# Delta rule and MLP on one core: squares of two chunks, one V scaling and three weight exponents at other places of the start-up

## The chip, the core and the metric

The kernel runs on one core of a Trainium2 chip. The core has five engines that work side by side, each through its own list of instructions in order: TensorE (PE, matmuls, and PEld for its weight loads), VectorE (DVE), ScalarE (ACT), GpSimd (POOL) and SyncE (SP), whose queue issues most of the DMA transfers. They wait for each other on semaphores. The metric is the device time of one execution in microseconds (us).

## The reference

All arrays are float32. The first half is a delta rule over 768 time steps for 4 batches of 8 heads with head size 48; its output is laid out as 3072 tokens of 384 numbers and goes through an MLP with the exact GELU.

```python
k_n = k / (np.linalg.norm(k, axis=-1, keepdims=True) + 1e-06)
for t in range(S):                       # S = 768
    y[:, :, t] = np.einsum('bhd,bhde->bhe', q[:, :, t], state)
    v_old = np.einsum('bhde,bhd->bhe', state, kt)
    state = state + bt * np.einsum('bhd,bhe->bhde', kt, vt - v_old)
x = y.transpose(0, 2, 1, 3).reshape(3072, 384)
h = x @ w_in                             # 384 x 2048
out = (0.5 * h * (1.0 + erf(h / sqrt(2)))) @ w_out   # 2048 x 384
```

The caller hands `moe_w_in` and `moe_w_out` over as 64-bit floats; the kernel makes 32-bit floats of their bits itself.

## The kernel before

**Tiling.** The 768 steps are cut into 12 chunks of 64. A *unit* is one chunk of two batches (128 partitions: two batches by 64 steps; 8 heads along the free axis), so a chunk has two units. Chunks go in pairs, called groups: group 0 is chunks 0 and 1, group 1 is chunks 2 and 3. `first` holds the four units of group 0, `third` the two of chunk 2, `fourth` the two of chunk 3.

**One group.** K is transposed on PE (`transposed`, copied to SBUF by ACT as Kt), its Gram matrices are made (`grams`, PE; copied by ACT as G and diag), and for every head a triangular system of 64 rows is inverted: 32-row diagonal blocks by row steps on DVE (`eliminate_steps`, lines 442 and 444: 60 short instructions for one group), the off-diagonal block by two small products (`join`, psJ on PE). The result is Zf. Its halves are written by DVE transposes (L457), by ACT copies (L499), and the quarters that must be zero by memsets on POOL (L466), the first of them by ACT (L464). The norms of K come from sums of squares: by DVE for group 0, and for group 1 by `sum_of_squares` (L291): one ACT instruction for each unit and head that squares 128x48 numbers and adds them up along the way. `prep` takes the root of these sums on POOL (L306, `pow`), `finish_both` (DVE) makes factors of them.

**One chunk.** `against_state` makes the right-hand side W (for chunk 0 from V alone, on POOL, L562; later with psK from PE), `solve` multiplies it by Zf (psU on PE, copied to U by ACT, L603), `use` makes the output and the state's update (psY on PE), `read` copies the output to x (ACT, L636, four instructions for a unit), `next_state` adds the update to the state St (DVE, L629), `turn` transposes x on PE for the MLP (copied by ACT as xT, L660). `queries` makes the products of Q and K, called P; for chunks 0 and 1 `masked` (POOL, L405) masks them. `scale_v` (POOL, L332) multiplies V by the norms of K.

**The MLP.** `fc1` makes a 128-column group of the hidden layer (psH, L677: six matmul instructions on PE) and its GELU on ACT (L679, tile G); there are 16 such groups for a chunk and two PSUM buffers for them. `fc2` is the second layer (psO, L690); from chunk 2 on it is done in seven products (L715).

**The weights.** They come in 16 parts, eight of w_in and eight of w_out. Part n is decoded in four steps, five DVE instructions and one ACT instruction: `begin(n)` (DVE, L218) takes the exponent bits, `exponents(n)` (ACT, L223) clamps and scales them, `mantissas(n)` (DVE, L228 and L230) makes the mantissas, `signed(n)` (DVE, L235 and L236) joins both and releases the raw buffer, on which `fetch` (SP, L210) loads a later part. The raw parts of w_in lie in w_out's space (four buffers), those of w_out in three others; the exponents (w_e) have two buffers.

**What sets the order.** Up to the first `next_state` everything is written out by hand: there the order of the calls in the program is the order on every engine. Behind that, steps get a due time in units of a chunk (`plan`); DVE keeps exactly that order, and on the other engines a planner places the instructions by its own estimates. The hand-written part is, in short: loads; squares, transposes and diagonals of group 0; Grams of group 0; transposed Q and queries of the four units; transposes and Grams of chunks 2 and 3; the row steps (which run on DVE all that while); `against_state` and the four masks on POOL; the joins, with the DVE transposes between them; then V of chunk 1 is scaled and the first parts of the weights are decoded around `solve`, `use` and `read` of chunk 0.

In the planned part the 32 sums of squares are due from 1.08 to 1.5, among the weights' parts 3 to 10 and the hidden layer of chunk 0. For chunk 3, K lies twice in SBUF: in Kp, where it is loaded late, and in Qp[2] and Qp[3], where it is loaded early for the transposes.

Of the kernel before, what the change touches and what calls it, by code (L numbers as in the profile page):

```python
# [8 lines left out]
F32 = mybir.dt.float32  # L9
# [3 lines left out]
ACT = mybir.ActivationFunctionType  # L13
# [3 lines left out]
def kernel(  # L17
# [28 lines left out]
    nc = tc.nc  # L46
# [152 lines left out]
    def fetch(n):  # L199
        if n >= len(w_parts):  # L200
            return
        dst, src = w_parts[n]
        if n < n_in:
            raw = stage[:, n % NS * 2 * WG:(n % NS + 1) * 2 * WG]
        else:
            raw = slots[(n - n_in) % len(slots)]
        w_raw[n] = raw.rearrange("q (n w) -> q n w", w=2)
        raw = raw.rearrange("q (m n w) -> q m n w", m=dst.shape[1], w=2)
        for m in range(dst.shape[1]):
            nc.sync.dma_start(out=raw[:, m], in_=src[:, m])  # L210
# [10 lines left out]
    def exponents(n):  # L221
        e = halves[n][3]
        nc.scalar.activation(e, e, ACT.Relu, bias=lim[:, 0:1], scale=float(2 ** 23))  # L223

    def mantissas(n):
        dst, lo, hi, e = halves[n]
        bits = dst.bitcast(U32)
        nc.vector.tensor_scalar(bits, hi, 0xFFFFF, 0x100000, op0=ALU.bitwise_and,  # L228
                                op1=ALU.bitwise_or)
        nc.vector.scalar_tensor_tensor(dst, lo, 2.0 ** -32, bits, ALU.mult, ALU.add)  # L230
# [52 lines left out]
    def sum_of_squares(u, h):  # L283

        if "both" not in ns:
            n23 = wk.tile([128, 2 * NA, H], F32, tag="n0", name="n0", bufs=1)
            ns[2], ns[3] = n23[:, 0:NA], n23[:, NA:]
            ns["both"] = n23
        if h == 0:
            u.ksq = wk.tile([128, H, D], F32, tag="ksq", name="ksq")  # L290
        nc.scalar.activation(u.ksq[:, h], u.Kn[:, h, 0:D], ACT.Square,  # L291
                             accum_out=ns[u.c][:, u.a, h:h + 1])

    def prep(c):
# [36 lines left out]
    def scale_v(u, engine=nc.gpsimd):  # L331
        engine.tensor_tensor(u.V, u.V, ns[u.c][:, u.a].unsqueeze(2).to_broadcast([128, H, D]),  # L332
                                op=ALU.mult)

    def transposed(u, part=(0, 1)):
        for x in part:
            if x == 0:
                dst = u.Kt = wk.tile([128, 2, NP, C], F32, tag="Kt", name="Kt", bufs=6)
            elif u.c == 1:
                dst = u.Qt = su.tile([128, 2, NP, C], F32, tag="Qt1", name="Qt1")  # L340
            else:
                dst = u.Qt = wk.tile([128, 2, NP, C], F32, tag="Qt", name="Qt")
            psT = sq("psT", NP, 128)
            flat = (Qp[2 + u.a] if u.c == 3 and x == 0 else (u.Kp, u.Qp)[x]).rearrange("q h d -> q (h d)")
            for j in range(NP):
                nc.tensor.transpose(psT[:, j, :], flat[:, j * 128:(j + 1) * 128], ident)
            nc.scalar.copy(dst.rearrange("q p j n -> q j p n"),
                           psT.rearrange("q j (p n) -> q j p n", p=2))
# [23 lines left out]
    def grams(us):  # L372
        g = us[0].c // 2
        psG = products(us, 0)
        if us[0].t == 0:
            Gs[g] = (wk if g else su).tile([128, NU, HB], F32, tag="G", name="G", bufs=1)
        span = slice(us[0].t * H, (us[-1].t + 1) * H)
        nc.scalar.copy(heads(Gs[g][:, span]), psG[:, :, :, HB:C])
        if g > 0:
            if us[0].t == 0:  # L380
                Ds[g] = wk.tile([128, NU, HB], F32, tag="diag", name="diag", bufs=1)
            nc.scalar.copy(heads(Ds[g][:, span]), psG[:, :, :, 0:HB])
            for p in range(2):
                lower = slice(p * C + HB, (p + 1) * C)
                nc.scalar.copy(Ds[g][lower, span], Gs[g][lower, span])
# [3 lines left out]
    def queries(us):  # L389
        c = us[0].c  # L390
        psP = products(us, 1)
        if c not in Ps:
            Ps[c] = (su if c == 1 else wk).tile([128, NA * H, C], F32, tag=f"P{c == 1}", name="P",
                                                bufs=1)
        for u in us:
            u.P = Ps[c][:, u.a * H:(u.a + 1) * H]
        dst = heads(Ps[c][:, us[0].a * H:(us[-1].a + 1) * H])
        if c < 2:
            nc.scalar.copy(dst, psP)
        else:  # L400
            both = mask.unsqueeze(1).to_broadcast([128, len(us) * H, C])
            nc.vector.tensor_tensor(dst, psP, heads(both), op=ALU.mult)  # L402
# [411 lines left out]
    def signs(c0, c1):  # L814
        psB = sq("psB", c1 - c0, B * H)
        for c in range(c0, c1):
            nc.tensor.transpose(psB[:, c - c0, :], bt[:, c].rearrange("n p t -> n (p t)"),
                                ident[0:B * H, 0:B * H])
        for p in range(2):
            src = psB[HALF[p]].rearrange("q c (a p h) -> q c a p h", p=2, h=H)[:, :, :, p, :]  # L820
            nc.scalar.mul(beta_m[HALF[p], c0:c1], src, -1.0)
# [27 lines left out]
    for u in first:  # L849
        grams([u])  # L850
    signs(2, NC)
    for u in first:
        transposed(u, (1,))
        queries([u])
    for a in range(NA):
        fetch_in(tiles[2, a].Qp[:, :, 0:D], q, tiles[2, a])
# [1 line left out]
        fetch_in(Qp[2 + a][:, :, 0:D], k, tiles[3, a])  # L858
    for n in range(2, NS):
        fetch(n)  # L860
    for n in range(n_in, n_in + len(slots)):
        fetch(n)
    load_v(1)
    third = [tiles[2, a] for a in range(NA)]
    for u in third:
        transposed(u, (0,))
    grams(third)
    for u in third:
        transposed(u, (1,))
    fourth = [tiles[3, a] for a in range(NA)]  # L870
    for u in fourth:
        transposed(u, (0,))
    grams(fourth)
    for fn, *args in rows:
        fn(*args)
    nc.vector.scalar_tensor_tensor(ng, gms[0][:, 0:NA], -1.0, ns[0], ALU.mult, ALU.mult)
    back0[0](*back0[1:])
    against_state(first[:NA])
    for u in first:
        masked(u)  # L880
    back1[0](*back1[1:])
    for a in range(NA):
# [1 line left out]
    back2[0](*back2[1:])  # L884
    for a in range(NA):
        join(0, (a,), 1)
    for u in first[NA:]:
        scale_v(u)
    begin(0)
    exponents(0)  # L890
    mantissas(0)
    begin(1)
    mantissas(1)
    solve(first[:NA])
    exponents(1)
    signed(0)
    use(first[:NA])
    for u in first[:NA]:
        read(u)
    signed(1)  # L900
    for u in first[:NA]:
        turn(u)
    for u in first[:NA]:
        update(u)
    begin(2)
    exponents(2)
    mantissas(2)
    signed(2)
    for u in first[:NA]:
# [7 lines left out]
    def late():  # L917
# [3 lines left out]
        for a in range(NA):  # L921
# [3 lines left out]
            for c in range(5, NC, 2):  # L925
# [4 lines left out]
    plan += [at(0.98, 0.985, [(1.0, load, 3)]),  # L930
             at(1.02, 1.1, [(1.0, join, 0, range(NA, 2 * NA), level) for level in range(2)]),
]
    sums = [(1.0, sum_of_squares, tiles[c, a], h) for c in (2, 3) for a in range(NA) for h in range(H)]
    plan += [at(1.08, 1.5, sums), at(1.51, 1.511, [(1.0, prep, c) for c in (2, 3)]), at(1.65, 1.655, [(1.0, finish_both)]), at(2.97, 2.971, [(1.0, finish, 4)]), at(2.675, 2.676, [(1.0, queries, third)]),
             at(1.12, 1.6, state_steps(1)),
             at(1.75, 2.45, eliminate_steps(1)),
             at(2.58, 2.74, join_steps(1)), at(2.72, 2.98, state_steps(2)),
# [75 lines left out]
```

## Time and profile before

Six runs had a median of 671.13 us (670.78 to 671.65).

| | |
|---|---|
| profiled execution, its own time | 670.97 us |
| its span | 669.3 us |
| mean granted clock of TensorE | 0.985 |
| PE busy | 642.4 us, 96% |
| DVE busy | 451.5 us, 67% |
| ACT busy | 229.3 us, 34% |
| POOL busy | 82.2 us, 12% |
| chain that ended last | PE 84%, DVE 10%, ACT 2% |

The shares are means over the whole span, and the stages differ. In the order of time:

| us | stage | DVE busy | ACT busy | POOL busy | PE busy |
|---|---|---|---|---|---|
| 47.00 to 51.80 | joins end, first parts decoded | 4.73 | 3.96 | 4.21 | 2.64 |
| 51.80 to 57.00 | solve, outputs of chunk 0 | 5.08 | 4.99 | 0.00 | 3.53 |
| 57.00 to 62.13 | turn, update, first MLP group | 4.12 | 2.38 | 0.00 | 5.13 |
| 62.13 to 88.00 | hidden layer of chunk 0, parts 3 to 8 | 24.73 | 20.41 | 6.18 | 23.86 |
| 88.00 to 117.00 | parts 8 to 15, second layer of chunk 0 | 28.48 | 11.79 | 0.00 | 27.21 |

From 120 us to the end PE is busy 99% of the time. In the lines shown below, a row of the order of time has its start, its length, the engine, the line, the operation with the tiles it writes and reads and their sizes, and how many instructions are merged in the row; a bracket at the end is the idle time of the engine before it and what ended that. Starts of instructions on one engine can lie a little before the end of the one ahead, since they are pipelined.

### The profile page before, as it was taken

Reading aid. Unit: us, or ns where it says so; the run is one execution under the profiler, and the core shown is the slowest. Engines: PE = TensorE matmul, PEld = TensorE weight load, DVE = VectorE, ACT = ScalarE, POOL = GpSimd, SP = SyncE. Lnnn points to the kernel's source line nnn. Section 1 sums busy time; section 2 is a strip of 40 time slices with the busy share of each in tenths; the row PEclk is TensorE's granted clock in tenths of the full one; section 3 lists DMA queues with packets and bytes.
Section 4 is the critical chain, followed back from the end, with each engine's and each line's share of the span. In section 5 each row is a group of like instructions: output and inputs, shape, how many; then the busy total and the mean of one; then the engine's idle time right before and its main releaser. Section 6 shows DMA issues by size and latency. Waiting matters only on the chain.

```text
span 669.3 us, 21705 instructions
## 1 busy us (share of the span) xinstructions
PE 642.4 (96%) x9542; PEld 560.7 (84%) x9542; DVE 451.5 (67%) x921; ACT 229.3 (34%) x605; POOL 82.2 (12%) x82
## 2 busy tenths in 40 slices
PE   6868998999999999999999999999999999999997
PEld 5656775866789989989989989989989989989997
DVE  6999999994699846489846479845479844324021
ACT  3367754714342143142143142143142133122220
POOL 4050300104011021111021111021111010000000
PEclk9976999999999999999999999999999999999999
DMA  9786656203431232511332511212301210100101
GB/s 130 178 252 172 118 171 134 48 0 69 81 50 37 49 51 43 87 27 32 55 50 48 85 26 28 52 21 34 65 3 24 56 19 3 24 2 2 24 1 25
DMA packets 158431, 39.76 MB, mean 59 GB/s; under 512 B 150016, under 2 KB 153216, under 8 KB 158336
## 3 DMA queue, kind: packets, MB, share of 16 engines
q1 hardware_dynamic: 152464, 33.40, 26.3%
q10 hardware_dynamic: 5872, 4.97, 3.2%
q8 instruction: 75, 1.23, 0.8%
q14 instruction: 20, 0.16, 0.1%
HBM read 33.62 MB, written 4.72 MB: 57 GB/s over the span
## 4 chain that ended last, share of the span: by engine, by line
PE 84%; DVE 10%; ACT 2%; issue 2%; DMA 1%; SPq 0%; DVEq 0%; ACTq 0%
PE psH L677 36%; PE psX L715 12%; PE psY L715 12%; PE psZ L715 4%; PE psO L690 4%; PE psK L572 3%; PE psJ L517 3%; PE psG L367 3%; PE psU L597 2%; PE psY L615 2%; DVE tmp L442 2%; DVE Nu L444 2%; DVE w_e L235 1%; PE psY L624 1%; DVE w_out_sb L236 1%
## 5 line engine op out<-in xcount | busy, mean ns | idle before, releaser
L677 PE MATMUL psH<-xT,w_in_sb 128*128 128x256 f32 x1152 | 262.2, 384 | 1.8 <-ACT G L679 1.7
L677 PEld LDWEIGHTS psH<-xT,w_in_sb 128*128 128x128 f32 x1152 | 216.0, 191 | 33.3 <-ACT G L679 3.3
L679 ACT ACTIVATE G<-psH 128x256 f32<-128x256 f32 x192 | 73.5, 383 | 180.2 <-PE psH L677 168.2
L444 DVE TENSOR_TENSOR Nu<-Nu,tmp 128x30 f32<-128x30 f32 (+9 forms) x180 | 62.9, 349 | 6.2
L442 DVE TENSOR_TENSOR tmp<-Nu 128x30 f32<-128x30 f32 (+9 forms) x180 | 60.5, 336 | 5.1
L715 PE MATMUL psX<-w_out_sb,G 128*128 128x192 f32 x320 | 56.2, 329 | 0.0
L715 PE MATMUL psY<-w_out_sb,G 128*128 128x192 f32 x304 | 54.2, 329 | 0.6
L715 PEld LDWEIGHTS psX<-w_out_sb,G 128*128 128x128 f32 x320 | 52.2, 190 | 0.7
L715 PEld LDWEIGHTS psY<-w_out_sb,G 128*128 128x128 f32 x304 | 49.1, 190 | 2.1 <-DVE u L761 1.8
L690 PE MATMUL psO<-w_out_sb,G 128*128 128x384 f32 x128 | 45.4, 496 | 1.6 <-DVE w_out_sb L236 1.6
L660 ACT COPY xT<-psX 128x384 f32<-128x384 f32 x24 | 11.4, 478 | 102.6 <-PE psX L659 101.5
L306 POOL TENSOR_TENSOR n<-n,half 128x16 f32<-128x16 f32 x10 | 29.4, 2938 | 86.4 <-DVE n L281 65.4
L690 PEld LDWEIGHTS psO<-w_out_sb,G 128*128 128x128 f32 x128 | 23.0, 190 | 17.3 <-DVE w_out_sb L236 4.0
L603 ACT COPY U<-psU 64x192 f32<-64x192 f32 x96 | 30.1, 314 | 20.6 <-PE psU L597 19.4
L402 DVE TENSOR_TENSOR P<-psG,mask 128x1024 f32<-128x1024 f32 x10 | 12.2, 1224 | 34.9 <-PE psG L367 34.9
L466 POOL MEMSET Zf<- 32x512 f32 x23 | 12.4, 540 | 154.1 <-DVE Zf L457 153.2
L724 DVE TENSOR_TENSOR S<-G 128x512 f32<-128x512 f32 x20 | 13.7, 687 | 25.8 <-ACT G L679 25.7
L580 DVE TENSOR_TENSOR W<-psK,V 128x384 f32<-128x384 f32 x22 | 12.2, 553 | 28.1 <-ACT y L579 28.1
L332 POOL TENSOR_TENSOR V<-V,n 128x384 f32<-128x384 f32 x18 | 17.3, 964 | 108.0 <-DMA V<-in_v_dram 95.4
L638 DVE TENSOR_TENSOR x<-psY,y 64x192 f32<-64x192 f32 x80 | 28.2, 353 | 0.9
L715 PE MATMUL psY<-T,G 128*128 128x192 f32 x160 | 28.2, 329 | 0.0
L715 PE MATMUL psX<-T,G 128*128 128x192 f32 x160 | 28.1, 329 | 0.0
(138 smaller groups left out, 869.0 us busy)
## 6 DMA issues: line engine op xcount, KB each, us to landing
Kp<-in_k_dram SPq DMA_DIRECT2D x76, 96.0 KB, 3.6
w_out_sb<-in_moe_w_in_dram SPq DMA_DIRECT2D x24, 256.0 KB, 3.8
V<-in_v_dram SPq DMA_DIRECT2D x48, 96.0 KB, 3.0
out_dram<-o_sb ACTq DMA_DIRECT2D x46, 96.0 KB, 2.2
w_raw<-in_moe_w_out_dram SPq DMA_DIRECT2D x10, 384.0 KB, 5.3
Zf<-in_moe_w_out_dram SPq DMA_DIRECT2D x6, 384.0 KB, 6.6
Qp<-in_q_dram SPq DMA_DIRECT2D x64, 32.0 KB, 2.2
Qp<-in_q_dram SPq DMA_DIRECT2D x16, 96.0 KB, 3.9
```

What stands on the lines that cost most here:

```text
L306: nc.gpsimd.tensor_tensor(flat, flat, half, op=ALU.pow)
L367: nc.tensor.matmul(psG[HALF[p], r, i * NP + j, :], lhsT=u.Kt[rows, p, j, :], rhs=(u.Qt if x else u.Kt)[rows, p, j, :], start=True, stop=True)
L442: nc.vector.tensor_tensor(tmp, nu[:, j + 1:, j:j + 1].to_broadcast([128, n, j]), nu[:, j:j + 1, 0:j].to_broadcast([128, n, j]), op=ALU.mult)
L444: nc.vector.tensor_tensor(nu[:, j + 1:, 0:j], nu[:, j + 1:, 0:j], tmp, op=ALU.add)
L517: nc.tensor.matmul(psJ[to, i, :], lhsT=(xm if level else off)[rows, u, :], rhs=zf[rows, u, HB:C] if level else xm[rows, u, :], start=True, ...
L572: nc.tensor.matmul(u.psK[to, x, r, j, :], lhsT=(u.Qt if x else u.Kt)[rows, p, j, :], rhs=St[rows, u.a, p, j, :], start=True, stop=True)
L603: copy(pairs(u.U[HALF[p]], s), u.psU[HALF[p ^ s], p])
L638: nc.vector.tensor_tensor(dst, src, pairs(u.y[HALF[p ^ s]], s), op=ALU.add)
L677: nc.tensor.matmul(psH, lhsT=w_in_sb[:, f // 2, m, f % 2 * 128:(f % 2 + 1) * 128], rhs=xTs[c][:, m, :], start=(m == 0), stop=(m == NM - 1))
L679: nc.scalar.activation(G[:, f, :], psH, ACT.Gelu)
L690: nc.tensor.matmul(u.psO, lhsT=G[:, f, u.a * 128:(u.a + 1) * 128], rhs=w_out_sb[:, f, :], start=(f == 0), stop=(f == NF - 1))
L715: nc.tensor.matmul(ps_, lhsT=lhs[:, f, :], rhs=rhs[:, f, :], start=first and f == 0, stop=f == FH - 1, skip_group_check=not first)
```

## The change

Three things are placed elsewhere:

- The 32 sums of squares of chunks 2 and 3 go from the planned part into the hand-written one: eight of chunk 2 between the transposes and the queries of the last two units of `first` (four for each), eight behind the transposes of chunk 2's K, and the sixteen of chunk 3 behind chunk 3's Grams. Those of chunk 3 read K from Qp[2] and Qp[3]. Their sums lie in a tile that takes turns with another (`root` in place of `n0`).
- V of chunk 1 is scaled on POOL between the masks of chunk 0 and those of chunk 1, so before the memsets of Zf. Its loads go out ahead of the first loads of w_out.
- `exponents(1)` stands ahead of `solve` on ACT; `begin(2)` stands behind `signed(0)` on DVE, and `exponents(2)` between the reads of the two units of chunk 0.

In the planned part the instructions of the other engines fall in another order behind that. On ACT the exponents of part 8 stand behind the GELUs of groups 11, 12 and 13; before, behind 11 and 12. On PE one matmul pair of group 11 comes between the two halves of psU of chunk 1.

```diff
     def sum_of_squares(u, h):
         if "both" not in ns:
-            n23 = wk.tile([128, 2 * NA, H], F32, tag="n0", name="n0", bufs=1)
+            n23 = wk.tile([128, 2 * NA, H], F32, tag="root", name="n23", bufs=1)
...
-        nc.scalar.activation(u.ksq[:, h], u.Kn[:, h, 0:D], ACT.Square,
+        kn = Qp[2 + u.a] if u.c == 3 else u.Kn
+        nc.scalar.activation(u.ksq[:, h], kn[:, h, 0:D], ACT.Square,
                              accum_out=ns[u.c][:, u.a, h:h + 1])
...
+    third = [tiles[2, a] for a in range(NA)]
+    some = iter([(u, h) for u in third for h in range(H)])
     for u in first:
         transposed(u, (1,))
+        for i in range(4 if u.t > 1 else 0):
+            sum_of_squares(*next(some))
         queries([u])
...
     for n in range(2, NS):
         fetch(n)
+    load_v(1)
     for n in range(n_in, n_in + len(slots)):
         fetch(n)
-    load_v(1)
-    third = [tiles[2, a] for a in range(NA)]
     for u in third:
         transposed(u, (0,))
+    for left in some:
+        sum_of_squares(*left)
     grams(third)
...
     grams(fourth)
+    for u in fourth:
+        for h in range(H):
+            sum_of_squares(u, h)
     for fn, *args in rows:
         fn(*args)
...
-    for u in first:
+    for u in first[:NA]:
+        masked(u)
+    for u in first[NA:]:
+        scale_v(u)
+    for u in first[NA:]:
         masked(u)
...
-    for u in first[NA:]:
-        scale_v(u)
     begin(0)
     exponents(0)
     mantissas(0)
     begin(1)
     mantissas(1)
+    exponents(1)
     solve(first[:NA])
-    exponents(1)
     signed(0)
+    begin(2)
     use(first[:NA])
-    for u in first[:NA]:
-        read(u)
+    read(first[0])
+    exponents(2)
+    read(first[1])
     signed(1)
...
-    begin(2)
-    exponents(2)
     mantissas(2)
     signed(2)
...
-    sums = [(1.0, sum_of_squares, tiles[c, a], h) for c in (2, 3) for a in range(NA) for h in range(H)]
-    plan += [at(1.08, 1.5, sums), at(1.51, 1.511, [(1.0, prep, c) for c in (2, 3)]), ...
+    plan += [at(1.51, 1.511, [(1.0, prep, c) for c in (2, 3)]), ...
```

More of the change, by code (lines that the diff above doesn't have):

```diff
@@ L932 @@
 ]
-    sums = [(1.0, sum_of_squares, tiles[c, a], h) for c in (2, 3) for a in range(NA) for h in range(H)]
-    plan += [at(1.08, 1.5, sums), at(1.51, 1.511, [(1.0, prep, c) for c in (2, 3)]), at(1.65, 1.655, [(1.0, finish_both)]), at(2.97, 2.971, [(1.0, finish, 4)]), at(2.675, 2.676, [(1.0, queries, third)]),
+    plan += [at(1.51, 1.511, [(1.0, prep, c) for c in (2, 3)]), at(1.65, 1.655, [(1.0, finish_both)]), at(2.97, 2.971, [(1.0, finish, 4)]), at(2.675, 2.676, [(1.0, queries, third)]),
              at(1.12, 1.6, state_steps(1)),
```

## The prediction

> **What bounds the kernel now.** I read the page's chain of work that ended last, then the same chain piece by piece from 36 to 122 us, then the order of time of each engine there. From 119.88 us to the end the chain is TensorE almost without a break, work that the change doesn't touch, so what it moves must show before that. There the chain ends like this (start, length, what):
>
> ```profile
> 115.12 0.88 DVE w_e L235
> 116.02 0.97 DVE w_out_sb L236
> 117.03 2.85 PE psO L690 x8
> 119.88 2.59 PE psH L677 x12
> ```
>
> VectorE (DVE) decodes the weights to 116.98 us; eight matmuls wait for the last part. From 62.13 DVE has next to no gap, so whatever moves a DVE step there moves the end by the same amount. Its losses, from the order of time on DVE (start, length, engine, line; the bracket is the idle time before and what ended it):
>
> ```profile
> 47.49 0.96 DVE L228 TENSOR_SCALAR w_in_sb<-w_out_sb 128x768 uint32<-128x768 uint32 x1
> 49.83 1.19 DVE L228 TENSOR_SCALAR w_in_sb<-w_out_sb 128x768 uint32<-128x768 uint32 x1
> 51.05 1.47 DVE L230 SCALAR_TENSOR_TENSOR w_in_sb<-w_out_sb,w_in_sb 128x768 f32<-128x768 uint32 x1
> 56.76 0.55 DVE L228 TENSOR_SCALAR w_in_sb<-w_out_sb 128x768 uint32<-128x768 uint32 x1
> 59.22 0.96 DVE L235 SCALAR_TENSOR_TENSOR w_e<-w_out_sb,w_e 128x768 uint32<-128x768 uint32 x1 [0.91 <-ACT w_e L223]
> 87.99 0.96 DVE L235 SCALAR_TENSOR_TENSOR w_e<-Zf,w_e 128x768 uint32<-128x768 uint32 x1 [0.57 <-ACT w_e L223]
> ```
>
> Two waits for exponents on ScalarE (ACT), 0.91 and 0.57, and three steps longer than alone (0.55 and 0.96) beside GpSimd (POOL). The reader should see that at most some 3 us can be won. The work of ACT and POOL around it:
>
> ```profile
> 43.20 1.24 ACT L385 COPY diag<-G 32x512 f32<-32x512 f32 x2
> 47.28 0.63 ACT L464 ACTIVATE Zf<-low 32x512 f32<-32x512 f32 x1 [2.83 <-DVE Zf L457]
> 50.79 2.64 ACT L603 COPY U<-psU 64x192 f32<-64x192 f32 x8 [0.40 <-PE psU L597]
> 53.46 0.94 ACT L223 ACTIVATE w_e<-w_e,lim 128x768 uint32<-128x768 uint32 x1
> 65.78 0.23 ACT L291 ACTIVATE ksq<-Kp 128x48 f32<-128x48 f32 x1
> 67.14 0.37 ACT L679 ACTIVATE G<-psH 128x256 f32<-128x256 f32 x1
> 86.47 0.66 ACT L679 ACTIVATE G<-psH 128x256 f32<-128x256 f32 x2
> 87.02 0.94 ACT L223 ACTIVATE w_e<-w_e,lim 128x768 uint32<-128x768 uint32 x1
> 88.51 0.38 ACT L679 ACTIVATE G<-psH 128x256 f32<-128x256 f32 x1 [0.55 <-PE psH L677]
> 41.17 4.97 POOL L405 TENSOR_TENSOR P<-P,mask 128x512 f32<-128x512 f32 x4
> 47.30 2.18 POOL L466 MEMSET Zf<- 32x512 f32 x3 [1.16 <-DVE Zf L457]
> 49.56 2.14 POOL L332 TENSOR_TENSOR V<-V,n 128x384 f32<-128x384 f32 x2
> ```
>
> **The squares.** Six run from 65.78 to 67.14, 0.227 us each with their accumulator reads; 32 are moved. Two groups of four go between a Qt copy and a P copy of ACT, where it idles 1.25 us: 0.91 fits, no cost. Eight go behind the Kt copies, whose next free start is 33.97: they end at 35.79, and the G copy that started at 35.28 and all that alternates with TensorE behind it comes 0.51 later. The last sixteen stand behind the last diagonal copies, free at 44.33 (+0.51 = 44.84), and take 3.63, to 48.47. But the zeroing of Zf (L464), behind them in ACT's order, started at 47.28, on the chain. **It comes 1.19 late**; ACT had 2.83 idle here, and the squares need more. The joins on DVE may start some 0.2 later through the 0.51; the slack below covers that.
>
> **Exponents sooner.** ACT's order is now the Zf copies, exponents 0 and 1, U, the reads of the first unit, exponents 2, the other reads. Exponents 0 start at 49.45 + 1.19 = 50.64; from one to the next start is 0.84 (53.46 to 54.30), so U starts at 52.32 (psU is ready at 50.77 + 1.19 = 51.96), 1.53 late. U takes 2.67 to the next start: 54.99; four reads 1.30 (half of 54.30 to 56.91): 56.29; exponents 2: 57.13; four reads: 58.43. Before, the reads ended at 56.91: **TensorE's turn, update and first MLP group start 1.52 late**, the group at 59.66 + 1.52 = 61.18.
>
> On DVE the 0.91 wait goes: signed(2) is reached near 58.2 and exponents 2 are ready at 57.23. What is late next is the state sum L629, which waits for the update's end, 59.73 + 1.52 = 61.25. DVE is there, one sum done, at about 60.65 and waits 0.6. The next part begins near 61.77 against 62.13: of the 0.91 only **0.36** is won here.
>
> **V between the masks.** POOL does the same work in another order: two masks to 43.66, V to 45.80, two masks to 48.28, three memsets to about 50.5. The overlap cost DVE 0.40 (beside a memset) + 0.63 + 0.52 (beside V) = 1.55. Now DVE's first decode step meets a mask and the next ones memsets. No row shows that meeting; the bounds are 0, and 1.24 for a step held for a whole mask. I take 0.64, as beside V, the nearest row, and 0.40 for each of two memsets: 1.44, a gain of 0.1, swallowed by the 0.6 of slack at the state sum; a loss of up to 0.6 would be, too. The first memset ends near 49.0, before psU's start, 48.76 + 1.19 = 49.95. V's DMAs are issued from 34.13 instead of 39.08, ahead of six weight loads on SyncE's (SP's) queue; they landed 6.1 to 7.4 us after issue, so the first pair by about 42 and the second by 44.5, needed at 43.66 and 44.73. The weight loads issue some 4 us later and are first read at 84.94: free.
>
> [...]
>
> **From 62 to 88 us.** The 7.3 us of squares leave ACT, so TensorE loses its waits for Gelu outputs (0.86, 0.31, 0.50). Its new course, by lengths of the old: the first MLP group, 2.72 at half clock, to 63.90; joins 1.13; two groups of 1.345, to 67.72; a group with joins 2.48; three groups, to 74.23; psK 2.01; four groups 5.38, to 81.62. That is 1.02 ahead of the old 82.64. But the changed order of ACT puts exponents 8 behind *three* Gelus after U, not two. psU with a third of a group between its halves ends for U at 81.62 + 1.21 + 0.45 = 83.28; the first Gelu comes 2.62 after that, 85.90; the third group starts 0.44 later (it needs that buffer), its Gelu 1.60 later at 87.94, exponents 8 at 88.22, and DVE's step 0.97 later, at **89.19**. It stood at 87.99. DVE, ready at 87.06, waits 2.1 us instead of 0.57. Behind it DVE has no gap to give back up to 116.98, and TensorE, ahead of it, still waits there.
>
> Sum: no other term reaches the end, which moves by 89.19 - 87.99 = **+1.20 us**. Against the profiled execution's own 670.97 us (span 669.3 and 1.7 around it) that is 672.17; that execution lay 0.16 under the median of 671.13, so 672.3.
>
> **The clock is the open term.** The granted clock was 0.50 from 45.2 to 62.10, then 1.00. TensorE had been busy without a gap since 56.94, 5.2 us. I let the rise come 1.52 later with the same work (63.62). In the other rise, at 41.65, half clock had lasted only 3.3 to 3.4 us: that soon after 58.43 the rise comes at 61.8, and half of 1.8 us is saved: +0.3. Twice that stretch gives 65.2: +2.0. [...]
>
> **Rivals.**
> - *The rise is early and the shift nearly hidden:* +0.0 to +0.6, 671.1 to 671.7. For it: the short stretch before 41.65. Against: 5.2 us the second time.
> - *The rise is late, or V lands late:* each makes TensorE's chain longer. +1.8 to +2.4, 672.9 to 673.5. V costs only once the second pair lands past about 45.5, since the memset has 0.9 to spare; against it 7.4 at most in the trace.
> - *Faster:* the squares hide wholly in ACT's idle 2.83. If they ended before 47.28, the chain would not be late, and DVE would win 0.91 + 0.57 and most of V's 1.15: 668.5 to 669.7. It decides below 0.15 us a square in place of 0.227; the row speaks against it. That the exponents aren't the last thing DVE waits for is in the forecast.
>
> **How the numbers follow.** Forecast (+0.6 to +1.8) 0.50; early rise 0.20; late 0.20; faster 0.10. A measurement of this kernel can hardly tell less than 0.2%, 1.34 us, from no change. The forecast's part above +1.34 is 0.20 and joins the late case: slower 0.40; the rest of it and the early case: same 0.50; faster 0.10. The range 670.9 to 673.3 leaves out the fast case and the ends of the late one.
>
> **What would show it.** The Zf zeroing on ACT near 48.5 directly behind squares; U near 52.3; no wait at signed(2), one of about 0.6 at L629; then TensorE without Gelu waits from 64 to 75; a wait of some 2 us on DVE for L223 near 87 to 89; the last w_out step at about 118.2. Wrong if exponents 8 come in time: then the DVE wait near 87 is short and the end is early. Wrong the other way if POOL holds psU (memset past 50) or squares wait for their DMAs.

## The result, and the profile after

The changed kernel took 673.02 us (median of 19 runs, 672.10 to 674.36), the kernel before 671.02 (39 runs): a ratio of 1.0029, 95% interval 1.0023 to 1.0035. It is slower by 2.0 us. The range on record (670.9 to 673.3) holds that. The likeliest outcome, within 0.2%, is not what came; slower by over 0.2% had a chance of 0.4.

The profiled execution after took 673.26 us (span 671.5), 2.29 more than the one before. The fences below show single rows of a view; rows between them are left out. The chain of waits of the changed kernel, in order of time (start, length, what):

```profile
48.56 0.63 ACT Zf L465
...
87.76 1.58 PE psH L678 x6
...
89.74 0.83 ACT w_e L223
90.60 0.97 DVE w_e L235
...
118.62 0.97 DVE w_out_sb L236
119.63 2.85 PE psO L691 x8
122.48 2.59 PE psH L678 x12
```

The last decode step starts at 118.62 where it stood at 116.02. DVE's step for part 8 moved just as much, from 87.99 to 90.60, and everything behind it kept its distance: psO follows 29.03 after that step (29.04 before). Back from that step the chain runs over ACT and TensorE without a break to the zeroing of Zf at 48.56. So the question of the whole study is what sets the step of part 8. In the order of time of the changed kernel, ACT:

```profile
48.56 0.63 ACT L465 ACTIVATE Zf<-low 32x512 f32<-32x512 f32 x1
50.74 1.76 ACT L223 ACTIVATE w_e<-w_e,lim 128x768 uint32<-128x768 uint32 x2
52.52 2.64 ACT L604 COPY U<-psU 64x192 f32<-64x192 f32 x8
...
84.71 2.59 ACT L604 COPY U<-psU 64x192 f32<-64x192 f32 x8 [1.55 <-PE psU L598]
87.32 0.66 ACT L680 ACTIVATE G<-psH 128x256 f32<-128x256 f32 x2
89.36 0.38 ACT L680 ACTIVATE G<-psH 128x256 f32<-128x256 f32 x1 [1.38 <-PE psH L678]
89.64 0.93 ACT L223 ACTIVATE w_e<-w_e,lim 128x768 uint32<-128x768 uint32 x1
```

Zf's zeroing has lost its idle 2.83 in front and starts at 48.56 instead of 47.28: squares stand directly ahead of it. Further down, the exponents of part 8 are behind a third Gelu, which itself waits 1.38 for TensorE. TensorE in the same view:

```profile
61.39 2.93 PE L678 MATMUL psH<-xT,w_in_sb 128*128 128x256 f32 x6
64.25 1.44 PE L485 MATMUL psJ<-XM,G 32*32 32x32 f32 x64
...
82.66 0.68 PE L598 MATMUL psU<-W,Zf 64*64 64x48 f32 x32
83.27 0.70 PE L678 MATMUL psH<-xT,w_in_sb 128*128 128x256 f32 x2
83.90 0.68 PE L598 MATMUL psU<-W,Zf 64*64 64x48 f32 x32
...
87.76 1.56 PE L678 MATMUL psH<-xT,w_in_sb 128*128 128x256 f32 x6 [0.82 <-ACT G L680]
```

The first hidden-layer group starts 1.73 later than before (59.66) and runs wholly at half clock (0.50 until 64.86). psU starts at 82.66, where it was before (82.64), but is split around a pair of group 11. The kernel before, TensorE and ACT:

```profile
59.66 2.79 PE L677 MATMUL psH<-xT,w_in_sb 128*128 128x256 f32 x6
82.64 1.15 PE L597 MATMUL psU<-W,Zf 64*64 64x48 f32 x64
83.85 2.59 ACT L603 COPY U<-psU 64x192 f32<-64x192 f32 x8 [0.72 <-PE psU L597]
```

So U starts 0.86 later than before (84.71 against 83.85), and from U's start to the exponents of part 8 it is 4.93 instead of 3.17 (83.85 to 87.02). Together that is 2.62, all that step 8 moved. VectorE and GpSimd of the changed kernel:

```profile
47.70 1.06 DVE L218 TENSOR_SCALAR w_e<-w_out_sb 128x768 uint32<-128x768 uint32 x1
48.68 0.96 DVE L228 TENSOR_SCALAR w_in_sb<-w_out_sb 128x768 uint32<-128x768 uint32 x1
51.02 0.58 DVE L228 TENSOR_SCALAR w_in_sb<-w_out_sb 128x768 uint32<-128x768 uint32 x1
58.28 0.95 DVE L235 SCALAR_TENSOR_TENSOR w_e<-w_out_sb,w_e 128x768 uint32<-128x768 uint32 x1
60.67 0.56 DVE L630 TENSOR_TENSOR St<-St,psY 128x384 f32<-128x384 f32 x1 [0.45 <-PE psY L625]
61.60 0.55 DVE L630 TENSOR_TENSOR St<-St,psY 128x384 f32<-128x384 f32 x1 [0.37 <-PE psY L625]
90.60 0.96 DVE L235 SCALAR_TENSOR_TENSOR w_e<-Zf,w_e 128x768 uint32<-128x768 uint32 x1 [3.25 <-ACT w_e L223]
...
45.84 2.50 POOL L406 TENSOR_TENSOR P<-P,mask 128x512 f32<-128x512 f32 x2
48.40 2.27 POOL L467 MEMSET Zf<- 32x512 f32 x3
50.75 3.12 POOL L307 TENSOR_TENSOR n<-n,half 128x16 f32<-128x16 f32 x1
```

The wait of 0.91 for exponents 2 is gone (58.28 has no bracket); 0.45 and 0.37 for the state's update take its place; and the wait for the exponents of part 8 has grown from 0.57 to 3.25. The steps that overlapped GpSimd cost 0.51 + 0.41 + 0.03 over their length alone (0.55 each), 0.95 in place of 1.55.

### The profile page after: what moved, and what is told of

Same layout as the page of the kernel before. It is cut to its first block, busy times and chain, and to the rows that moved or that the text cites. A ratio compares the mean times of both kernels' runs of the same rounds, so it can differ in the third digit from the quotient of the medians.

```text
span 671.5 us, 21714 instructions
## 1 busy us (share of the span) xinstructions
PE 644.2 (96%) x9542; PEld 562.1 (84%) x9542; DVE 451.8 (67%) x921; ACT 229.7 (34%) x605; POOL 81.9 (12%) x82
## 3 DMA queue, kind: packets, MB, share of 16 engines
q8 instruction: 75, 1.23, 0.8%
## 4 chain that ended last, share of the span: by engine, by line
PE 89%; DVE 4%; ACT 4%; issue 2%; DMA 1%; SPq 0%; ACTq 0%
PE psH L678 38%; PE psX L716 12%; PE psY L716 12%; PE psG L368 4%; PE psZ L716 4%; PE psO L691 4%; PE psK L573 3%; PE psJ L518 3%; PE psU L598 2%; PE psT L347 2%; PE psY L616 2%; PE psY L625 1%; DVE w_out_sb L236 1%; DVE w_e L235 1%; PE psX L660 1%
## 5 line engine op out<-in xcount | busy, mean ns | idle before, releaser
L445 DVE TENSOR_TENSOR Nu<-Nu,tmp 128x30 f32<-128x30 f32 (+9 forms) x180 | 61.8, 344 | 6.2
L443 DVE TENSOR_TENSOR tmp<-Nu 128x30 f32<-128x30 f32 (+9 forms) x180 | 61.7, 343 | 5.1
L467 POOL MEMSET Zf<- 32x512 f32 x23 | 12.5, 544 | 153.8 <-DVE Zf L458 152.8
```

What stands on the lines that cost most here:

```text
L443: nc.vector.tensor_tensor(tmp, nu[:, j + 1:, j:j + 1].to_broadcast([128, n, j]), nu[:, j:j + 1, 0:j].to_broadcast([128, n, j]), op=ALU.mult)
L445: nc.vector.tensor_tensor(nu[:, j + 1:, 0:j], nu[:, j + 1:, 0:j], tmp, op=ALU.add)
```

## The experiments

One sum holds for ten of the twelve profiles. "Step 8" is the start of DVE's product for part 8; the last column but one is that execution's own time less this start. A median belongs to all runs, the rest to one execution, which need not be a typical one. A ratio is to the kernel before as it ran beside each kernel (medians 670.77 to 671.02), so it isn't the quotient of two medians of this table.

| kernel | Zf zeroed | step 8 [wait for ACT] | own time | own time - step 8 | median, ratio to before |
|---|---|---|---|---|---|
| before | 47.28 | 87.99 [0.57] | 670.97 | 582.98 | 671.02 |
| changed | 48.56 | 90.60 [3.25] | 673.26 | 582.66 | 673.02, 1.0029 (1.0023 to 1.0035) |
| V alone | 47.38 | 89.08 [1.52] | 671.71 | 582.63 | 671.72, 1.0013 (1.0004 to 1.0022) |
| squares alone | 48.69 | 90.46 [1.60] | 673.27 | 582.81 | 672.70, 1.0034 (1.0021 to 1.0046) |
| exponents alone | 47.27 | 86.97 [0.58] | 669.38 | 582.41 | 669.83, 0.9985 (0.9977 to 0.9994) |
| changed, exponents 8 first | 48.15 | 87.38 [0.19] | 670.18 | 582.80 | 671.59, 1.0009 (1.0000 to 1.0017) |
| changed, no early squares | 47.14 | 89.56 [2.94] | 671.93 | 582.37 | 671.42, 1.0008 (1.0000 to 1.0017) |
| both of these | 47.46 | 87.02 [0.48] | 670.07 | 583.05 | 670.13, 0.9985 (0.9977 to 0.9994) |
| chunk 3's squares twice | 51.58 | 93.46 [3.13] | 675.97 | 582.51 | 676.12, 1.0074 (1.0060 to 1.0087) |
| extra matmuls | 48.21 | 89.22 [2.25] | 677.48 | 588.26 | 674.69, 1.0060 (1.0037 to 1.0083) |
| chunk 2's squares early only | 46.98 | 88.79 [2.74] | 672.49 | 583.70 | 672.04, 1.0019 (1.0010 to 1.0028) |
| chunk 3's squares early only | 48.00 | 88.98 [2.18] | 671.91 | 582.93 | 672.31, 1.0022 (1.0013 to 1.0030) |

In ten of twelve the remainder is 582.4 to 583.1. Apart from the two exceptions, told below, the step of part 8 tells the time to within 0.7 us.

**V alone** (the kernel before with V of chunk 1 scaled between the masks, and its loads earlier).

```diff
+    load_v(1)
     for n in range(n_in, n_in + len(slots)):
         fetch(n)
-    load_v(1)
...
-    for u in first:
+    for u in first[:NA]:
+        masked(u)
+    for u in first[NA:]:
+        scale_v(u)
+    for u in first[NA:]:
         masked(u)
...
-    for u in first[NA:]:
-        scale_v(u)
```

> Only V of chunk 1 and its loads are moved; squares and exponents stand as before. In this program, too, ACT has the exponents of part 8 behind three Gelus after U, and psU has a third of an MLP group between its halves. Theory 'order' (the exponents of part 8 come too late because of what stands ahead of them on ACT and PE): TensorE reaches psU as before at 82.6 us, U starts 2.0 later, the third Gelu comes 4.65 after that, DVE's step 1.24 after the Gelu, at about 90.5 instead of 88.0: 673.2 us, ratio 1.0033. Rival 'squares' (the zeroing of Zf, held up by sixteen squares, is what costs): nothing is held up here, 671.0. Rival 'contention' (V beside DVE's decode): a gain of up to 1.2, 669.8.

Measured: 671.72 us, between the 673.2 of 'order' and the 671.0 of 'squares'. DVE reached the product for part 0 at 51.88 instead of 52.44, so V between the masks is worth 0.56 there. It was given back: waits for exponents of 0.68 and 0.92 on the next two products, and the start of part 3 at 62.22 against 62.13. TensorE reached psU at 81.20, not near 82.6: its waits for Gelus and for DVE's XM came to 0.74 in place of 1.67, and its first hidden-layer group took 2.18 to the next start in place of 2.72 (the clock rose near 61.2 and not at 62.2, an estimate from the row's length: 2.25 here, 2.93 in the changed kernel, at half clock to its end, and 2.11 with exponents 8 first, where the rise came 1.2 after its start). That part of the expectation was wrong. The loss comes at part 8: with the squares and the exponents untouched the planner already put the third Gelu ahead of exponents 8, and DVE waited 1.52 there. V's place is enough to bring that order. So are the squares alone, as the next run shows; only the kernel before and the exponents alone keep two Gelus there.

**Squares alone** (the kernel before with the 32 sums early).

```diff
     for u in first:
         transposed(u, (1,))
+        for i in range(4 if u.t > 1 else 0):
+            sum_of_squares(*next(some))
         queries([u])
...
     grams(fourth)
+    for u in fourth:
+        for h in range(H):
+            sum_of_squares(u, h)
```

> Only the 32 squares are moved. The zeroing of Zf comes 1.2 us late and the first MLP group starts near 60.9 us instead of 59.7; ACT has the exponents of part 8 behind three Gelus. Theory 'order': DVE's step for part 8 at 89.2 to 90.0 us, 672.2 to 673.0. Rival 'squares': the end is late by what Zf is late, 672.2, and the wait at part 8 stays near 0.6. Rival 'the chunk as a whole gains, the V move costs': below 671.0.

Measured: 672.70 us, as bad as the whole change. Zf is zeroed at 48.69, the waits for exponents 1 and 2 remain (0.93 and 0.92), and exponents 8 are late by 1.60. Here, too, three Gelus stand ahead of exponents 8. Of the 2.47 that step 8 comes late, 1.44 are there when part 3 starts (63.57 against 62.13), and 1.03 are the longer wait at part 8 (1.60 against 0.57). So the end is late by Zf and by the order. The median lies in the range of 'order' (672.2 to 673.0), the step 0.5 beyond it. The squares are enough for the whole loss, and what the other two parts win and lose about cancels.

**Exponents alone** (the kernel before with exponents 1 and 2 sooner).

```diff
     begin(1)
     mantissas(1)
+    exponents(1)
     solve(first[:NA])
-    exponents(1)
     signed(0)
+    begin(2)
     use(first[:NA])
-    for u in first[:NA]:
-        read(u)
+    read(first[0])
+    exponents(2)
+    read(first[1])
     signed(1)
...
-    begin(2)
-    exponents(2)
     mantissas(2)
```

> Only the exponents of parts 1 and 2 are moved. ACT keeps two Gelus ahead of the exponents of part 8. Theory 'order': the 0.91 wait goes, U starts 0.5 late, DVE gains up to 0.9 at part 3 and loses it again at part 8, whose exponents come 0 to 0.5 late: 671.0 to 671.5, ratio 1.000 to 1.0007. Rival 'DVE alone sets the end': the 0.9 is kept, 670.1, ratio 0.9987.

Measured: 669.83 us, faster by 0.15%. My theory gave this part less; the rival won, that DVE alone sets the end here. The order of time on DVE, exponents alone:

```profile
58.20 0.95 DVE L235 SCALAR_TENSOR_TENSOR w_e<-w_out_sb,w_e 128x768 uint32<-128x768 uint32 x1
60.18 1.02 DVE L629 TENSOR_TENSOR St<-St,psY 128x384 f32<-128x384 f32 x2
61.11 0.55 DVE L218 TENSOR_SCALAR w_e<-w_out_sb 128x768 uint32<-128x768 uint32 x1
86.97 0.96 DVE L235 SCALAR_TENSOR_TENSOR w_e<-Zf,w_e 128x768 uint32<-128x768 uint32 x1 [0.58 <-ACT w_e L223]
```

No wait is left before the state's sum, which finds its data there; part 3 begins 1.02 sooner than the 62.13 of before, and the step of part 8 stands 1.02 sooner. The 0.91 is won in full here: nothing of it is taken back at the state's sum, as the prediction had it. That wait comes with the squares, and in part with V (0.37 without any early square, below), not with the exponents.

Step 8 itself still waits 0.58 for ACT, so DVE's gain has to reach ACT too. It does so through TensorE, first in the kernel before, then with the exponents alone:

```profile
67.98 1.19 PE L484 MATMUL psJ<-Zf,XM 32*32 32x32 f32 x62 [0.31 <-DVE XM L495]
66.96 1.19 PE L484 MATMUL psJ<-Zf,XM 32*32 32x32 f32 x62 [0.31 <-DVE XM L495]
```

TensorE waits for a tile of DVE (XM) in both, and from there on TensorE, U and exponents 8 all stand 1.02 sooner, though the first hidden-layer group started 0.45 later (60.11 against 59.66).

**The changed kernel with exponents 8 first** (two Gelus held behind the exponents).

```diff
-        nc.scalar.activation(e, e, ACT.Relu, bias=lim[:, 0:1], scale=float(2 ** 23))
+        marks[n] = nc.scalar.activation(e, e, ACT.Relu, bias=lim[:, 0:1], scale=float(2 ** 23))
...
-        nc.scalar.activation(G[:, f, :], psH, ACT.Gelu)
+        behind = {(0, 13): 8, (0, 14): 9}.get((c, f))
+        with tc.issue_after(marks[behind].ins) if behind else ExitStack():
+            nc.scalar.activation(G[:, f, :], psH, ACT.Gelu)
```

> The changed kernel, with only ACT's order altered: the Gelu of group 13 is put behind the exponents of part 8 and the Gelu of group 14 behind those of part 9. Squares, V and early exponents stay as changed. Theory 'order': exponents 8 start 0.6 us after U ends (87.9 in the changed kernel's time) instead of 89.64, DVE's step comes 1.7 earlier: 671.3 us, ratio 1.0004 against the kernel before. Rival 'squares': the late Zf sets the end whatever stands later: 672.6 to 673.0, ratio 1.0025 or more.

Measured: 671.59 us, 1.4 less than the changed kernel, near the 671.3 of 'order' and below the 672.6 of its rival. In the order of time of this kernel:

```profile
85.86 0.66 ACT L682 ACTIVATE G<-psH 128x256 f32<-128x256 f32 x2
86.41 0.94 ACT L223 ACTIVATE w_e<-w_e,lim 128x768 uint32<-128x768 uint32 x1
...
87.38 0.96 DVE L235 SCALAR_TENSOR_TENSOR w_e<-Zf,w_e 128x768 uint32<-128x768 uint32 x1 [0.19 <-ACT w_e L223]
```

The exponents stand behind two Gelus again, 3.16 after U's start instead of 4.93, and DVE waits 0.19. Step 8 of this execution is 3.22 sooner than the changed kernel's; the rest of that is an earlier Zf (0.41) and an earlier rise of the clock (62.1 against 64.9). This profiled execution is the fastest of the eleven; the gain is read from the medians.

**No early squares** (the changed kernel, with the sums back in the plan).

```diff
-        for i in range(4 if u.t > 1 else 0):
-            sum_of_squares(*next(some))
...
-    for u in fourth:
-        for h in range(H):
-            sum_of_squares(u, h)
...
+    sums = [(1.0, sum_of_squares, tiles[c, a], h) for c in (2, 3) for a in range(NA) for h in range(H)]
+    plan += [at(1.08, 1.5, sums), ...
```

> The changed kernel with the sums of squares back where the planner put them before; V between the masks and the early exponents stay. Theory (the sixteen squares in front of Zf are the loss, and the ScalarE order at the exponents of group 8 is a second, smaller one): Zf's last copy ends near 47.3 to 47.9 us, next part begins at 60.7 to 61.3 with no wait in front of the second and third product of the exponents' chain, but VectorE still waits 1.5 to 2 us for the exponents of group 8 behind three Gelus; the earlier start of about 1.0 and that wait cancel: 670.6 to 671.4 us, ratio 0.999 to 1.001. Rival (the squares are hidden, the order at group 8 is everything): within 0.3 us of the changed kernel, 672.7 to 673.3, ratio 1.003.

Measured: 671.42 us, ratio 1.0008, at the upper edge of what the theory gave (670.6 to 671.4). Zf is back at 47.14, part 3 begins at 60.90, and DVE still loses 2.94 waiting for exponents 8 behind the third Gelu (in this execution the clock rose only at 64.0). Without the squares the two other parts neither win nor lose much.

**Both** (no early squares, and exponents 8 ahead of Gelu 11, exponents 9 ahead of Gelu 13).

```diff
+        behind = {(0, 11): 8, (0, 12): 8, (0, 13): 9}.get((c, f))
+        with tc.issue_after(marks[behind].ins) if behind else ExitStack():
             nc.scalar.activation(G[:, f, :], psH, ACT.Gelu)
```

> The kernel of the run before this, and two more edges in ScalarE's order: the exponents of group 8 stand ahead of the Gelu of column block 11, those of group 9 ahead of that of block 13. Theory: VectorE's step for part 8 waits less than 0.3 us and stands near 86.5 us, against 87.99 with 0.57 before: early exponents give 1.0, V between the masks gives 0.5, the lost wait 0.3 to 0.5: 668.7 to 669.4, ratio 0.997. Rival 1 (TensorE's state sum sets the start of the next part, so V's half microsecond is lost there): as the early exponents alone, 669.8, ratio 0.9985. Rival 2 (Gelus held back make TensorE late): over 671.

Measured: 670.13 us, ratio 0.9985, the same as the exponents alone; my theory (668.7 to 669.4) was wrong and the first rival right. Against the changed kernel the ratio falls by 0.0020 with the order alone, by 0.0021 without early squares, and by 0.0044 with both: the late Zf and the third Gelu are two losses that add up, within intervals of some 0.0009 each way (the two edits of ACT's order differ in the Gelus that they hold). The order of time, ACT and then DVE:

```profile
49.64 2.02 ACT L223 ACTIVATE w_e<-w_e,lim 128x768 uint32<-128x768 uint32 x2
51.68 2.63 ACT L603 COPY U<-psU 64x192 f32<-64x192 f32 x8
...
59.83 0.55 DVE L629 TENSOR_TENSOR St<-St,psY 128x384 f32<-128x384 f32 x1
60.75 0.56 DVE L629 TENSOR_TENSOR St<-St,psY 128x384 f32<-128x384 f32 x1 [0.37 <-PE psY L624]
61.22 0.55 DVE L218 TENSOR_SCALAR w_e<-w_out_sb 128x768 uint32<-128x768 uint32 x1
87.02 0.96 DVE L235 SCALAR_TENSOR_TENSOR w_e<-Zf,w_e 128x768 uint32<-128x768 uint32 x1 [0.48 <-ACT w_e L223]
```

DVE is 0.43 ahead of the exponents-alone kernel at the product for part 0 (52.00 against 52.43), and then waits 0.37 at the state's sum. The chain through U is now late instead: U starts at 51.68, against 51.23 there and 50.79 before. Of these 0.45, 0.19 are there at Zf's zeroing, and 0.26 come from DVE. The step `begin(1)`, on which exponents 1 wait, starts 0.72 later than with the exponents alone (first row: both corrections; second: exponents alone):

```profile
50.07 0.55 DVE L218 TENSOR_SCALAR w_e<-w_out_sb 128x768 uint32<-128x768 uint32 x1
49.35 0.55 DVE L218 TENSOR_SCALAR w_e<-w_out_sb 128x768 uint32<-128x768 uint32 x1
```

About 0.5 of that is the first decode step, which takes 1.07 beside a mask where it took 0.56. So the two exponents take 2.02 together (1.76 there), and ACT has no gap from 47.46 to 58.3 but this one. Exponents 1 ahead of U and V between the masks get in each other's way here: V's half microsecond lands in the wait at the state's sum.

**Chunk 3's squares twice** (the changed kernel, these sixteen run a second time).

```diff
-    for u in fourth:
+    for u in fourth + fourth:
```

> The changed kernel with the sixteen squares of chunk 3 run twice in a row in front of Zf, so that only their number differs: 16 x 0.227 = 3.63 us more of ScalarE there. Theory (this place is on the path): Zf's last copy ends near 52.2 instead of 48.6, the two exponents behind it too, the first product of the next part waits; the time rises by most of it: 675.5 to 677, ratio 1.007 to 1.009. Rival (ScalarE has slack there and only its order at group 8 costs): at most 673.5, ratio 1.003 to 1.004.

Measured: 676.12 us. Zf is zeroed at 51.58, 3.02 after the changed kernel's 48.56; step 8 is 2.86 later. On DVE:

```profile
54.72 0.96 DVE L235 SCALAR_TENSOR_TENSOR w_e<-w_out_sb,w_e 128x768 uint32<-128x768 uint32 x1 [2.54 <-ACT w_e L223]
93.46 0.96 DVE L235 SCALAR_TENSOR_TENSOR w_e<-Zf,w_e 128x768 uint32<-128x768 uint32 x1 [3.13 <-ACT w_e L223]
```

ACT work in front of Zf's zeroing is on the path: of 3.63 us added, 3.1 show in the median. The rival, that ACT has room there, is out.

**Chunk 2's squares early, and chunk 3's early, each alone** (changed kernel; the other sixteen go back to the plan). In the first, chunk 3's planned squares read from Qp, which holds other rows by then, so these sums, and with them the output, are of other numbers; instructions and sizes are the same, and only the time is used.

> The changed kernel with chunk 2's sixteen squares early, as changed, and chunk 3's back in the plan. Theory (the loss is an overflow: ScalarE has about 4.0 us free ahead of Zf where no square stands there, and the two halves together need more): Zf's last copies go at 47.1 to 47.7 on time, the rest is as without any early square: 671.0 to 671.9 us, ratio 1.000 to 1.0015. Rival (the squares between the row steps themselves cost, since the copy of G and what follows on TensorE come 0.3 to 0.9 later): 672.2 to 672.8, ratio 1.002 to 1.003.

> The changed kernel with chunk 3's sixteen squares early, as changed, and chunk 2's back in the plan. Theory (overflow): ScalarE is free at 43.1 as without any early square, 16 x 0.227 = 3.63 us of squares end at 46.75, before VectorE has Zf's input at 47.1, so Zf is on time within 0.3: 671.2 to 672.0 us, ratio 1.000 to 1.0015, and only the two halves together cost. Rival (chunk 3's squares stand on the path by themselves): Zf at 48.0 or later, 672.4 to 673.0, ratio 1.0025 to 1.003.

Measured: 672.04 and 672.31 us. Both medians lie just above the theory's ranges and below the rivals'. In the profiles the theory that only both together overflow ACT's room fell for chunk 3. The order of time, chunk 3's squares only:

```profile
38.14 1.97 PE L347 MATMUL psT<-ident,Qp 128*128 128x128 f32 x8 [2.06 <-ACT Qt L348]
48.00 0.63 ACT L465 ACTIVATE Zf<-low 32x512 f32<-32x512 f32 x1
```

I had counted on ACT being free at 43.1, read from the kernel without early squares, where these eight transposes took 1.15 at full clock. Here the clock had fallen to 0.50 at about 38.1, they took 1.97, ACT was free at 44.25, and the sixteen squares ended at 47.98. The room ahead of Zf is not a constant: ACT's idle there measured 2.79 (chunk 2's squares only), 2.83 (before), 3.23 (exponents alone), 3.50 (both corrections), 3.68 (V alone) and 4.01 (no early squares); the last two had these transposes at full clock, in 1.15. The sixteen squares' 3.63 us fit only there.

Chunk 2's squares alone leave Zf on time (46.98, after 2.79 of idle), and step 8 at 88.79 is even sooner than without early squares; but the clock rose at 61.9 in the one execution and at 64.0 in the other. That its median is still 0.6 above that kernel's is not explained by these steps: the intervals overlap, and its profiled execution loses 0.33 between step 8 and psO behind a DMA of raw weights that took 6.01 us, and 0.69 in an idle of TensorE (psG) for which the profile names no releaser and which was 0.47 before. This stays open.

**Extra matmuls** (the changed kernel; nine products of the identity with itself on TensorE, six ahead of `solve`, one behind it, two between the two turns; their result is read by nobody).

```diff
+    def busy(n):
+        psW = sq("psW", NP, 128)
+        for i in range(n):
+            nc.tensor.matmul(psW[:, i % NP, :], lhsT=ident, rhs=ident, start=True, stop=True)
...
+    busy(6)
     solve(first[:NA])
+    busy(1)
...
+    turn(first[0])
+    busy(2)
+    turn(first[1])
```

> The changed kernel with nine extra matmuls of the identity with itself in TensorE's three idle stretches of the exponents' chain (six ahead of U's solve, one behind it, two between the two transposes); their result is read by nobody, they are work added only to keep TensorE's granted clock from falling or to bring its rise forward. Theory (the phase of the clock's rise sets a term of 1 to 2 us): the clock is up before the first group of the feed-forward product at 61.4, which then takes 1.4 to 2.0 instead of 2.9 us, and VectorE's step for part 8 stands near 88.5 to 89.5 instead of 90.6: 670.8 to 672, ratio 0.9995 to 1.0015. Rival (the clock plays no part, ScalarE's order alone sets it): 672.7 to 673.5, ratio 1.003.

Measured: 674.69 us, with a spread from 670.22 to 679.15 that no other kernel had: inconclusive on the question it was made for. Locally it looked as the theory wanted: the clock rose near 62.3, the first hidden-layer group took 2.16, step 8 stood at 89.22, 1.38 sooner. But in this execution the clock had fallen and risen within 0.1 us of the times before the change (38.4, 41.8, 45.2 us), not as in the changed kernel's profile (41.0), so the early rise may belong to that other course of the clock and not to the added work. Kernels without that work rose as early (61.7 with the exponents alone, 62.1 with exponents 8 first). And 5.6 us were lost far behind, in a place that the extra matmuls do not touch. Windows of the extra-matmuls kernel (window, length, busy time and instructions of PE, PEld, DVE, ACT, POOL, then granted clock, DMA share, GB/s):

```profile
152.00:153.00 1.00, 1.00 (x122) 1.00 (x123) 0.00 (x0) 0.00 (x0) 0.70 (x2) 1.00 0.06 16
153.00:154.00 1.00, 0.17 (x18) 0.05 (x7) 0.00 (x0) 0.00 (x0) 0.00 (x0) 1.00 0.00 0
154.00:155.00 1.00, 0.00 (x0) 0.00 (x0) 0.00 (x0) 0.00 (x0) 0.00 (x0) 0.72 0.00 0
163.00:164.00 1.00, 1.00 (x3) 0.59 (x2) 0.00 (x0) 0.40 (x1) 0.00 (x0) 0.50 0.23 33
```

From 153.17 to 155.25 nothing ran on any engine; the clock was at 0.50 from about 154.4 to 164.7.

## Why the prediction was right, and where not

**Squares and Zf.** Right in the price, and to 0.2 in the steps: 0.227 us each, the sixteen from 44.82 (44.84 forecast), the last one over at 48.53 (48.47 forecast), the zeroing late by 1.28 (1.19 forecast), U at 52.52 (52.32), the first hidden-layer group at 61.39 (61.18). That the sixteen start on time to 0.02 is luck. I had ACT free at 44.33 in the profile of before, where the row gives 44.44 (43.20 + 1.24). The copy of G behind the eight earlier squares was 1.04 late (36.32 against 35.28), twice the 0.51 forecast, since the Kt copies had been 0.54 late already (34.03 against 33.49); and then eight transposes ran at full clock, in 1.15 instead of the 1.97 of before, and gave most of it back. In four executions with the same 32 squares Zf was zeroed at 48.15 to 48.69. That this place is on the path is shown by the doubled squares.

**Exponents sooner.** The steps came as told: no wait at the product for part 2, a wait for the state's sum (0.82 in two pieces, 0.6 forecast), part 3 at 62.07 (61.77 forecast, in an execution whose DVE decode began 0.67 late, 47.70 against 47.03, a scatter that spans 46.73 to 47.70 in all the profiles, with and without squares). What the prediction did not see is that the whole 0.91 and more is there for the taking when the exponents alone are moved (669.83).

**V between the masks.** Right that it brings nothing at the end, but for a wrong size: the overlap fell by 0.6, not by 0.1. The slack I named, the state's sum, did swallow it in the run with both corrections. Its cost, the changed order on ACT at exponents 8, was in the forecast but counted for the whole change; V alone brings it, and the squares alone do, too. And its hold on DVE's first step makes exponents 1, and with them U, late (0.26 with both corrections), which the forecast did not have. The first step took 1.06 beside a mask, from 47.70 to 48.76, where it takes 0.55 alone; the mask ended at 48.34, 0.42 ahead of it. The next step took 0.96 beside a memset, 0.41 over its length alone; the 0.58 and 0.55 beside the power instruction of 3.12 us show 0.03 at most.

**From 62 to 88 us.** The mechanism held: no Gelu wait on TensorE between 64 and 75, exponents 8 behind three Gelus, a wait of 3.25 (2.1 forecast). One reading was wrong: the 0.31 that I counted among the Gelu waits ends with DVE's XM (the row is shown with the exponents alone). Step 8 came at 90.60 instead of 89.19. The 1.41 is, to 0.02, the sum of four pieces (lengths from start to next start):

- 0.21: the first hidden-layer group starts later.
- 0.37: the clock, at half until 64.9 and not 63.62. The group took 2.86 for 2.72, the joins behind it 1.36 for 1.13.
- 0.46: the next six groups and the second joins, up to psK, took 9.66 for 9.20. It isn't the clock, since they took 9.65 at full clock with exponents 8 first. The new order on TensorE, groups in pieces of 14, 4 and 18 matmuls with joins between them, is the likely price; I had put it at nothing.
- 0.39: U starts 2.05 after psU begins, not 1.66. The pair between the halves of psU takes 0.63, and I had given it 0.45; the halves apart take 1.23 where psU in one piece took 1.08. These make 0.33 of it.

psK to psU (7.39) and U to exponents 8 (4.93 against 4.94) were exact. From step 8 on the distances held.

**The sum and the chances.** The median lies 0.7 above the 672.3, just above the forecast's own stretch (up to +1.8) and at the lower end of the late-rise rival (672.9 to 673.5). That rival's mechanism, a late rise, is in this profile, but for 0.37 only; TensorE's pieces (0.46) and the psU term (0.39) are as large. How many of the 19 runs rose late is not known. The early rise is out for this execution (64.9, not 61.8). The faster rival is out too: the squares do not fit. But a part of its price was real: 1.0 us, by the exponents alone (669.83 against 670.88 for the kernel before beside it).

**The clock.** In the profile of before the granted clock changed at 38.29, 41.70, 45.12 and 62.18, in the one after at 40.96 and 64.86. Half clock lasted 17.06 us in the first and 23.90 in the second, and some 20.4 with no early squares (43.6 to 64.0); ahead of the 17.06 stood 3.41 at half clock and 3.42 at full. The forecast let the rise come with the same amount of work behind TensorE's last idle. The profiles do not show that. Before, TensorE was busy from 56.94 and the rise came 5.24 later; in the changed kernel it was busy from 58.67 and the rise came 6.19 later; with chunk 3's squares only it was 3.8 (58.11 to 61.9, the rise estimated from the first group's 2.09 as with V alone), with no early squares 6.5 (57.50 to 64.0). What sets the moment of the rise these runs do not settle.

## What to carry to other kernels

Idle time of an engine right before an instruction on the path is not free room: add up the work to be put there (16 x 0.227 = 3.63) against the shortest idle seen there (2.8), not the longest (4.0), and look for an idle that ends in nothing on the path. When parts of a change are bundled, run them singly: here one part alone (669.83 us, the fastest kernel of the study) was hidden under the loss of another. Where a planner orders an engine's queue, look at that order around the next place where the bounding engine waits: the third Gelu ahead of exponents 8 cost 1.3 to 1.4 us and came with edits 40 us earlier that did not name it, with V's place as well as with the squares.

## What I had not expected of the hardware

- **Idle with no releaser.** TensorE stood still near 12.5 us for 0.53 before and 1.09 after (0.22 to 1.65 in the twelve profiles), and once more in the psJ products near 150 to 156 for about 0.6 in every kernel; in the kernel with extra matmuls a second such stop of 2.08 us follows there, with all engines idle. The view of what TensorE waited for, extra matmuls, from 146 to 168 us (total, times, longest):

```profile
PE psJ L518 <- issue: 2.7, 2, 2.1
```

  Why it is longer in that kernel no run here shows. The stop near 12.5 goes with the scatter at DVE's first decode step: that step starts at 46.73 to 46.93 in the three profiles with a stop below 0.3, at 46.95 to 47.12 in the four with 0.53 to 0.55, and at 47.21 to 47.70 in the five with 0.8 or more. How the one leads to the other was not traced.
- **A stop of 2.08 us, and half clock for 10 us.** Behind that stop TensorE was busy without a break from 155.25, and the granted clock still stood at 0.50 until 164.7 (it had fallen at 154.4). That is 9.4 us from the last idle to the rise, against 3.8 to 6.5 near 62 us; so being busy in the profile does not by itself tell when the clock rises. Near 62 us it rose 1.1 to 3.8 us after the start of the first hidden-layer group (62.1 after 60.98 with exponents 8 first, 64.0 after 60.22 without early squares). When the clock changes differs from execution to execution; in the changed kernel's profile the late rise makes the 0.37 above.
